# Rows of neighbouring tokens for the first two blocks of a fused channel-attention and SwiGLU kernel

## The chip, the cores and the metric

One core of a Trainium2 chip. The metric is the device time of one launch in microseconds, the median of the runs shown. The profile is one execution of the same program.

## The reference

```python
def _attn_ref(q, k, v, tau):
    qn = q / (np.linalg.norm(q, axis=1, keepdims=True) + 1e-06)
    kn = k / (np.linalg.norm(k, axis=1, keepdims=True) + 1e-06)
    s = kn.transpose(0, 2, 1) @ qn / tau
    s = s - s.max(-1, keepdims=True)
    a = np.exp(s)
    a /= a.sum(-1, keepdims=True) + 1e-09
    return (v @ a).astype(np.float32)

def _moe_ref(x, w_gate, w_val, w_out, rms_g):
    rms = np.sqrt(np.mean(x * x, axis=-1, keepdims=True) + 1e-06)
    xn = x / rms * rms_g
    g = xn @ w_gate
    silu = g * (1.0 / (1.0 + np.exp(-g)))
    val = xn @ w_val
    return (silu * val @ w_out).astype(np.float32)
```

There are two batches of 6016 tokens with 256 channels; the hidden layer has 1536 columns. q, k and v are fp32. The three weight matrices are float64 in HBM. The attention matrix is 256x256 for each batch and needs all of q and k of that batch; after it, every token stands alone.

## The kernel before

A tile is 128 tokens; a batch has 47 tiles. The work after the attention matrix runs in blocks of up to 4 tiles (`blocks`, BT = 4): eleven of 4 and one of 3 for each batch, 24 in all. The hidden layer is cut into 12 pieces of 128 columns (NF); a step is one block and one piece, (j, f). Every matmul on x, the weights and the hidden values is made of three fp32r products, of high parts and low parts (a high part is a rounding copy by ScalarE, its low part a subtraction).

**Start.** For batch 0 the scores s = k'q are summed on TensorE (`scores`, L174) over 15 chunks of q and k in three `raw` buffers, while ScalarE squares each chunk (`squares`, L189) and VectorE sums the squares (`add_squares`, L198). SP's queue loads q and k; the loads of a chunk are issued when the chunk three before it has been used. Between chunks the table `early` loads, decodes and splits the first weights: `load_w` brings a piece of all three matrices as 64-bit words (768 KB, two `wraw` buffers), `decode_w` makes fp32 of it by three operations of VectorE (L110, L119, L126) and one of ScalarE (L118), and `split_w` makes high parts (ScalarE, L134) and low parts (GpSimd, L136). v comes by `load_v` (L335) in four DMAs per block whose innermost run is 32 floats: tokens are dealt so that a VectorE transpose of 32x32 blocks (`move_v`, L366) gives v with channels on partitions. For blocks 0 and 1 these loads are issued from GpSimd's queue, the first as the first thing of the program. `split_v` makes high parts (L349) and low parts (L350, GpSimd).

**Softmax stage.** The norms, the softmax of batch 0 and the normed rows of block 0 follow: `norm_sums` (L216), `norms`, `inverse_norms`, `softmax_min`, `softmax_div`, `emit_x` (x = v a, tiles px, L386), `emit_x_squares`, `emit_xn`, `emit_xT_first` (L451). Scores of batch 1 fill TensorE's row between them (`fill`).

**Blocks 0 and 1** are plain (`emit_hidden`, L664, j < WINO = 2): six products each for pg and pv with the block's tokens as columns, then silu on ScalarE, the product hh on VectorE (L678), its high part gh on ScalarE (L553) and low part gl on GpSimd (L559). `emit_out` (L696) runs two steps later: three products per tile into po. pg and pv use four PSUM banks in turn. During block 0 the rest of batch 1's scores, and decoding and splitting of the weights of piece f + 3 and f + 2, are dealt over the steps (`weights`, `extra`).

**Blocks 2 to 23** use seven products where the plain form has eight (`new_products`, `emit_step`, L585). They need sums of weights: `build_s` makes them for pairs p of pieces in four parts i: VectorE adds high and low (part 0, L528), four additions (part 1, L537), ScalarE rounds (part 2, L540), VectorE subtracts (part 3, L543). Part i of pair p stands in step 12 + 2 + 3p + i, counted from block 0.

**Order.** The program is written by hand: an engine runs its instructions in the order written, and tables `ready0` to `ready` say in which step the next block's v, x and xT are made. With j = 0, `ready0` turns block 1's v in steps 1 and 2 (`v_moves`, `v_splits`) and makes px of block 1 at f = 4 and 6.

Of the kernel before, what the change touches and what calls it, by code (L numbers as in the profile page):

```python
# [15 lines left out]
P = 128  # L16
# [3 lines left out]
def kernel(  # L20
# [59 lines left out]
    def f32(ap):  # L80
        return ap.bitcast(F32)
# [50 lines left out]
    def split_w(f, piece=None):  # L132
        if piece in (None, 0):
            nc.scalar.activation(out=w_hl[0][:, f, :], in_=wval[f], func=AF.Copy)  # L134
        if piece in (None, 1):
            nc.gpsimd.tensor_tensor(  # L136
                out=w_hl[1][:, f, :], in0=wval.pop(f), in1=f32(w_hl[0][:, f, :]),
                op=ALU.subtract,
            )
# [188 lines left out]

    def load_v(j, queue=nc.sync):

        b, mu0, n = blocks[j]
        t = v_p.tile([P, A * BT, KC, S], F32, tag="v", name=f"v_{j}")
        src = v[b].rearrange("(s m) (c i r) -> i s m c r", s=S, c=KC, i=A)
# [5 lines left out]
        v_t[j] = t  # L339

# [96 lines left out]
    FIRST = 2  # L437

    def emit_xT_first(j, h):
# [6 lines left out]
        for c in range(KC):  # L446
# [207 lines left out]
    def emit_hidden(j, f, between=()):  # L654
# [28 lines left out]
        rounds.append((hh[:, :n], gh[:, :n], gl[:, :n], nc.gpsimd))  # L683
# [4 lines left out]
    def emit_out(j, f):  # L688
        b, mu0, n = blocks[j]
# [12 lines left out]
        if last:  # L702
# [5 lines left out]
            dst = out[b * N:(b + 1) * N, :].rearrange("(s m) e -> s m e", s=S)  # L708
            for a in range(A):
                if j < FIRST:  # L710
                    to = dst[:, mu0 + a * n:mu0 + (a + 1) * n, :]
                else:
                    to = dst[:, mu0:mu0 + A * n, :].rearrange("s (t a) e -> s t a e", a=A)[:, :, a, :]
                nc.sync.dma_start(out=to, in_=ob[S * a:S * (a + 1), :n, :])
# [3 lines left out]
    with tc.manual_schedule():  # L718
# [12 lines left out]
        load_v(0, nc.gpsimd)  # L731
# [10 lines left out]
        for i in range(6):  # L742
# [58 lines left out]
        norms(0)  # L801
        new_acc(1, 2)
# [42 lines left out]
        for f in range(NF):  # L845
# [3 lines left out]
            if f + 2 < NF:  # L849
                go.append(lambda f=f: split_w(f + 2))  # L850
# [84 lines left out]
        def rest(n):  # L935
# [30 lines left out]
            3: (then(2, v_moves),),  # L966
            4: (then(2, v_splits),),
# [84 lines left out]
```

## Time and profile before

| | us |
|---|---|
| median of 3 runs (lowest, highest) | 1321.57 (1321.02, 1322.63) |
| profiled execution, its own time | 1322.27 |
| its span, first to last instruction | 1320.4 |
| TensorE busy in the span (matmuls) | 1294.1 (98%) |
| VectorE, ScalarE, GpSimd busy | 686.1, 823.6, 679.3 |
| mean granted TensorE clock | 0.988 of full speed |

The profile shows each instruction of one execution. "Idle before" is the time an engine stood still ahead of an instruction, with what ended it. A busy TensorE is not TensorE at its peak: at half its clock it is as busy as at full.

### The profile page before, as it was taken

To read this page: it belongs to the slowest core of one execution; us is meant where nothing else is said; L and a number is where in the kernel's file an instruction comes from. 1 tells how busy PE (TensorE), PEld (TensorE's weight loads), DVE (VectorE), ACT (ScalarE), POOL (GpSimd) and SP (SyncE) were. 2 spreads that over 40 slices of the span, in tenths; PEclk is the share of its full clock that TensorE was granted. 3 is DMA by queue.
4 is the path that set the end of the run, shared out by engine and by line. 5 is a ranking of instruction groups with operands and counts; after the bars stand their busy time and mean duration, and the time that the engine had idled before them with its cause. 6 is when DMAs were issued, how large, how long until landed. Compare 5 with 4: busy or idle time off the path is not lost.

```text
span 1320.4 us, 26331 instructions
## 1 busy us (share of the span) xinstructions
PE 1294.1 (98%) x10212; PEld 1261.3 (96%) x10212; DVE 686.1 (52%) x1097; ACT 823.6 (62%) x1727; POOL 679.3 (51%) x616
## 2 busy tenths in 40 slices
PE   7999999899999999999999999999999999999998
PEld 6777888799999999999999999999999999999998
DVE  5679947753544543544643444444444444444443
ACT  4565655566657658656656666666666666666653
POOL 3226536266546546546546646646646646646432
PEclk8999999899999999999999999999999999999999
DMA  8956501202201201201201220220210210210100
GB/s 246 316 174 205 160 19 30 49 8 42 50 15 35 49 16 35 45 14 36 45 17 34 45 47 4 49 41 9 49 36 14 50 39 11 45 28 7 30 17 13
DMA packets 147678, 71.72 MB, mean 54 GB/s; under 512 B 100704, under 2 KB 139104, under 8 KB 147552
## 3 DMA queue, kind: packets, MB, share of 16 engines
q1 hardware_dynamic: 147168, 68.99, 20.3%
q0 software_dynamic: 384, 1.05, 0.5%
q8 instruction: 80, 1.31, 0.4%
q14 instruction: 46, 0.38, 0.1%
HBM read 46.40 MB, written 12.32 MB: 44 GB/s over the span
## 4 chain that ended last, share of the span: by engine, by line
PE 90%; DVE 4%; DMA 3%; ACT 1%; issue 1%; SPq 1%; ACTq 0%; DVEq 0%
PE pu L585 42%; PE po L696 29%; PE pq L585 7%; PE px L386 5%; PE s L174 3%; PE pg L664 2%; DMA raw<-in_k_dram 2%; PE pv L664 2%; DVE acc L198 1%; ACT sq L189 1%; DVE wx L119 0%; DMA raw<-in_q_dram 0%; DVE wk L537 0%; DVE s L543 0%; SPq L160 0%
## 5 line engine op out<-in xcount | busy, mean ns | idle before, releaser
L559 POOL TENSOR_TENSOR gl<-zg,gh 128x512 fp32r<-128x512 f32 (+1 forms) x262 | 327.5, 1271 | 421.5 <-ACT gh L553 220.1
L696 PE MATMUL po<-w,gh 128*128 128x256 f32 x2256 | 410.8, 280 | 0.0
L585 PE MATMUL pu<-xt,s 128*128 128x256 f32 (+1 forms) x2376 | 407.3, 280 | 0.5 <-ACT t L624 0.5
L619 ACT ACTIVATE t<-pu 128x512 f32<-128x512 f32 (+1 forms) x264 | 155.3, 588 | 372.5 <-DVE zv L613 195.2
L585 PE MATMUL pu<-xt,w 128*128 128x256 f32 (+1 forms) x2376 | 370.0, 282 | 6.2 <-DVE zg L612 5.3
L696 PEld LDWEIGHTS po<-w,gh 128*128 128x128 f32 x2256 | 348.0, 189 | 2.3 <-ACT gh L553 0.2
L585 PEld LDWEIGHTS pu<-xt,s 128*128 128x128 f32 x2376 | 336.1, 189 | 0.8 <-ACT t L624 0.7
L585 PEld LDWEIGHTS pu<-xt,w 128*128 128x128 f32 x2376 | 320.1, 189 | 7.4 <-DVE zg L612 5.9
L696 PE MATMUL po<-w,gl 128*128 128x256 f32 x1128 | 315.6, 280 | 0.1
L612 DVE TENSOR_TENSOR zv<-pu,t 128x512 f32<-128x512 f32 (+1 forms) x132 | 89.7, 680 | 336.9 <-ACT zg L632 150.4
L696 PEld LDWEIGHTS po<-w,gl 128*128 128x128 f32 x1128 | 212.9, 189 | 0.3 <-DVE gl L559 0.3
L612 DVE TENSOR_TENSOR zg<-pu,t 128x512 f32<-128x512 f32 (+1 forms) x132 | 89.7, 680 | 199.9 <-PE pu L585 189.9
L553 ACT ACTIVATE gh<-zg 128x512 fp32r<-128x512 f32 (+1 forms) x264 | 154.4, 622 | 7.3 <-DVE zg L628 4.6
L585 PE MATMUL pq<-xt,w 128*128 128x256 f32 (+1 forms) x792 | 136.1, 281 | 0.0
L628 DVE TENSOR_TENSOR zg<-zg,zv 128x768 f32<-128x768 f32 (+1 forms) x132 | 125.4, 950 | 14.4 <-DVE zv L613 0.9
L585 PEld LDWEIGHTS pq<-xt,w 128*128 128x128 f32 x792 | 111.7, 189 | 0.0
L626 ACT ACTIVATE zg<-zg 128x768 f32<-128x768 f32 (+1 forms) x132 | 109.0, 826 | 0.0
L174 PE MATMUL s<-raw 128*128 128x256 f32 x376 | 95.4, 412 | 10.6 <-DMA raw<-in_k_dram 10.6
L624 ACT ACTIVATE t<-pu 128x256 f32<-128x256 f32 (+1 forms) x264 | 100.0, 379 | 3.9 <-PE pu L585 1.3
L174 PEld LDWEIGHTS s<-raw 128*128 128x128 f32 x376 | 76.5, 208 | 25.6 <-issue 13.7
L198 DVE TENSOR_TENSOR acc<-acc,sq 128x1024 f32<-128x1024 f32 (+1 forms) x47 | 64.0, 1361 | 31.6 <-ACT sq L189 29.4
L386 PE MATMUL px<-a,vt 128*128 128x256 f32 x564 | 75.4, 283 | 0.0
(97 smaller groups left out, 1319.6 us busy)
## 6 DMA issues: line engine op xcount, KB each, us to landing
out_dram<-ob SPq DMA_DIRECT2D x88, 128.0 KB, 2.6
raw<-in_q_dram SPq DMA_DIRECT2D x20, 512.0 KB, 5.8
raw<-in_k_dram SPq DMA_DIRECT2D x20, 512.0 KB, 6.9
v<-in_v_dram SPq DMA_DIRECT2D x80, 128.0 KB, 3.8
xnT<-xw SPq DMA_DIRECT2D x320, 32.0 KB, 1.9
wraw<-in_moe_w_gate_dram SPq DMA_DIRECT2D x12, 256.0 KB, 3.5
wraw<-in_moe_w_val_dram SPq DMA_DIRECT2D x12, 256.0 KB, 4.0
wraw<-in_moe_w_out_dram SPq DMA_DIRECT2D x12, 256.0 KB, 4.8
```

The costliest lines, as they stand in the source:

```text
L174: nc.tensor.matmul(out=s_ps[b][:, c, :], lhsT=r[:, 1, t, c * P:(c + 1) * P], rhs=r[:, 0, t, :], start=(t0 + t == 0 and c == 0), stop=(t0 + ...
L198: engine.tensor_tensor(out=a, in0=a, in1=sq, op=ALU.add)
L386: nc.tensor.matmul(out=px[:, i, :], lhsT=w[:, c, t * P:(t + 1) * P], rhs=x[:, c, :], start=(i == 0 and c == 0 and m == 0), stop=(c == KC - ...
L553: nc.scalar.activation(out=gh, in_=hh, func=AF.Copy)
L559: engine.tensor_tensor(out=gl, in0=hh, in1=f32(gh), op=ALU.subtract)
L585: nc.tensor.matmul(out=out, lhsT=wm[wi], rhs=xm[xi], start=(start and q == 0), stop=(q == 2), skip_group_check=True,)
L612: nc.vector.tensor_tensor(out=z[:, 1:], in0=u, in1=t[:, :2], op=ALU.add)
L619: nc.scalar.activation(out=nt[:, 1:], in_=nu, func=AF.Copy)
L624: nc.scalar.activation(out=mt[:, 0], in_=mu[:, 1], func=AF.Copy)
L626: nc.scalar.activation(out=zg[:, 1:], in_=zg[:, 1:], func=AF.Silu)
L628: nc.vector.tensor_tensor(out=zg[:, 1:], in0=zg[:, 1:], in1=z, op=ALU.mult)
L696: nc.tensor.matmul(out=o_ps[j][t // 2][:, t % 2, :], lhsT=g[:, t * P:(t + 1) * P], rhs=wo[w][:, f, :], start=(first and t % 2 == 0 and m = ...
```

## The change

Tokens of blocks 0 and 1 are now neighbouring tokens of batch 0. Their v is loaded in rows by one DMA from SP's queue (`load_v_rows`, 3 or 4 KB a partition), turned by TensorE with the identity into PSUM (`turn_v`, tiles pvt) and split out of PSUM by ScalarE and VectorE (`split_turned`). Block 0 has 3 tiles in place of 4, and block 11 has 4 in place of 3. In block 0 the low parts gl and the low parts of the weights are made by VectorE. The first weights are loaded some chunks later, v of block 0 late in the chunks, v of block 1 after the softmax. The parts of `build_s` stand in other steps.

```diff
-    def split_w(f, piece=None):
...
-            nc.gpsimd.tensor_tensor(
-                out=w_hl[1][:, f, :], in0=wval.pop(f), in1=f32(w_hl[0][:, f, :]),
...
+    def split_w(f, engine=nc.gpsimd):
+        nc.scalar.activation(out=w_hl[0][:, f, :], in_=wval[f], func=AF.Copy)
+        engine.tensor_tensor(
+            out=w_hl[1][:, f, :], in0=wval.pop(f), in1=f32(w_hl[0][:, f, :]), op=ALU.subtract,
+        )
...
-            n = min(BT, NT - t)
+            n = (NT - t) % BT or BT if b == 0 else min(BT, NT - t)
...
+    def load_v_rows(j):
+        n = blocks[j][2]
+        v_t[j] = v_p.tile([P, A * BT, KC, S], F32, tag="v", name=f"v_{j}")
+        nc.sync.dma_start(
+            out=v_t[j].rearrange("p m c r -> p (m c r)")[:, :n * C],
+            in_=v[0, rows(j), :].rearrange("(p t) c -> p (t c)", p=P),
+        )
+
+    def turn_v(j, c, psum, tag):
+        n = blocks[j][2]
+        x = v_t[j].rearrange("p m c r -> p (m c r)")
+        v_w[j, c] = psum.tile([P, BN], F32, tag=tag, name=f"pvt_{j}_{c}")
+        for t in range(n):
+            nc.tensor.transpose(
+                v_w[j, c][:, t * P:(t + 1) * P], x[:, t * C + c * P:t * C + (c + 1) * P], ident
+            )
+
+    def split_turned(j, c):
+        n = blocks[j][2] * P
...
+        split(v_w.pop((j, c))[:, :n], [x[:, c, :n] for x in vT[j]])
...
-        rounds.append((hh[:, :n], gh[:, :n], gl[:, :n], nc.gpsimd))
+        rounds.append((hh[:, :n], gh[:, :n], gl[:, :n], nc.gpsimd if j else nc.vector))
...
-        load_v(0, nc.gpsimd)
...
         early = {
-            2: lambda: load_w(0),
-            5: lambda: (load_w(1), decode_w(0)),
-            6: lambda: split_w(0),
-            8: lambda: (load_w(2), decode_w(1)),
-            9: lambda: split_w(1),
-            12: lambda: load_w(3),
+            4: lambda: load_w(0),
+            7: lambda: (load_w(1), decode_w(0)),
+            8: lambda: split_w(0),
+            10: lambda: load_v_rows(0),
+            11: lambda: (load_w(2), decode_w(1)),
+            12: lambda: split_w(1),
+            13: lambda: load_w(3),
         }
...
-            if i == 3:
-                move_v(0, 0)
-                move_v(0, 1)
-                for c in range(KC):
-                    split_v(0, c, nc.gpsimd)
-                load_v(1, nc.gpsimd)
+        for c in range(KC):
+            turn_v(0, c, ps_gv, "u")
...
         norms(0)
+        for c in range(KC):
+            split_turned(0, c)
...
             softmax_div(0, c)
+        load_v_rows(1)
...
-                go.append(lambda f=f: split_w(f + 2))
+                go.append(lambda f=f: split_w(f + 2, nc.vector))
...
-        for i in reversed(range(4)):
+        at_step = [(2 * p + 2, 2 * p + 3, 2 * p + 3, 2 * p + 4) for p in range(NP - 2)]
+        at_step += [(10, 11, 12, 13), (15, 18, 19, 20)]
+        for i in (3, 0, 1, 2):
             for p in range(NP):
-                j, f = divmod(NF + 2 + 3 * p + i, NF)
+                j, f = divmod(NF + at_step[p][i], NF)
...
-            3: (then(2, v_moves),),
-            4: (then(2, v_splits),),
+            4: (then(2, v_moves),),
+            5: (then(2, v_splits),),
...
         ready0 = {
-            1: (v_moves,),
-            2: (v_splits,),
+            0: (turn(0),),
+            1: (turned(0),),
+            2: (turn(1),),
+            3: (turned(1),),
```

The output of blocks 0 and 1 goes out by one DMA in place of four (L708 to L714), and the loads and stores of batch 0's other blocks leave out the first 896 tokens. `ready2` moves block 4's v by one step.

**SP's queue in the first stage.** Of the kernel before, the loads behind chunk 5 (raw is q and k, wraw a piece of the weights):

```order
L96 DMA wraw_202<-in_moe_w_gate_dram 128x2x256
L96 DMA wraw_202<-in_moe_w_val_dram 128x2x256
L100 DMA wraw_202<-in_moe_w_out_dram 128x512
L160 DMA raw_6_220<-in_q_dram 128x1024
L160 DMA raw_6_220<-in_k_dram 128x1024
L160 DMA raw_7_251<-in_q_dram 128x1024
L160 DMA raw_7_251<-in_k_dram 128x1024
```

Of the change, the same place:

```order
L157 DMA raw_6_211<-in_q_dram 128x1024
L157 DMA raw_6_211<-in_k_dram 128x1024
L157 DMA raw_7_228<-in_q_dram 128x1024
L157 DMA raw_7_228<-in_k_dram 128x1024
L96 DMA wraw_231<-in_moe_w_gate_dram 128x2x256
L96 DMA wraw_231<-in_moe_w_val_dram 128x2x256
L100 DMA wraw_231<-in_moe_w_out_dram 128x512
```

The first weights stand behind two more chunks. The second piece moves from behind chunk 8 to behind chunk 10, the third from behind chunk 11 to behind chunk 14, the last of batch 0; v of block 0 stands between chunks 13 and 14.

**VectorE's row in block 0, one step.** Of the kernel before, step f = 0 (wx is a piece of weights in decoding, hh the hidden values, acc the sums of squares of batch 1):

```order
L110 TENSOR_SCALAR wx_608<-wraw_400 128x768
L678 TENSOR_TENSOR hh_0_606<-th_0_605,pv_0_598 128x512
L119 SCALAR_TENSOR_TENSOR wx_608<-wraw_400,wx_608 128x768
L126 SCALAR_TENSOR_TENSOR wx_608<-we_611,wx_608 128x768
L198 TENSOR_TENSOR acc_435<-acc_435,sq_2_2_629 128x1024
```

Of the change, the same step:

```order
L110 TENSOR_SCALAR wx_597<-wraw_393 128x768
L713 TENSOR_TENSOR hh_0_595<-th_0_594,pv_0_587 128x384
L119 SCALAR_TENSOR_TENSOR wx_597<-wraw_393,wx_597 128x768
L134 TENSOR_TENSOR w_101<-wx_534,w_100 128x768
L126 SCALAR_TENSOR_TENSOR wx_597<-we_600,wx_597 128x768
L594 TENSOR_TENSOR gl_0_611<-hh_0_595,gh_0_610 128x384
L195 TENSOR_TENSOR acc_432<-acc_432,sq_2_2_623 128x1024
```

Two operations are added to each step, the low parts of the weights (L134) and of the hidden values (L594), and GpSimd's row loses them. In steps 1 and 3 a subtraction for block 1's v (vt) follows behind gl.

**VectorE's row in block 1, two steps.** Of the kernel before, f = 4 to 6 (zh is the hidden product, wk and s are the parts of `build_s`, vw block 3's v):

```order
L678 TENSOR_TENSOR zh_4_1570<-zh_4_1570,pv_4_1563 128x512
L678 TENSOR_TENSOR zh_5_1606<-zh_5_1606,pv_5_1599 128x512
L543 TENSOR_TENSOR s_1439<-wk_1457,s_1438 128x512
L543 TENSOR_TENSOR s_1439<-wk_1457,s_1438 128x256
L543 TENSOR_TENSOR w_101<-wk_1457,w_100 128x256
L528 TENSOR_TENSOR wk_1612<-w_100,w_101 128x512 x2
L366 STREAM_TRANSPOSE vw_1631<-v_1148 128x4x4x32 x2
L678 TENSOR_TENSOR zh_6_1653<-zh_6_1653,pv_6_1646 128x512
```

Of the change:

```order
L713 TENSOR_TENSOR zh_4_1530<-zh_4_1530,pv_4_1523 128x512
L578 TENSOR_TENSOR s_1396<-wk_1414,s_1395 128x512
L578 TENSOR_TENSOR s_1396<-wk_1414,s_1395 128x256
L578 TENSOR_TENSOR w_101<-wk_1414,w_100 128x256
L563 TENSOR_TENSOR wk_1536<-w_100,w_101 128x512 x2
L713 TENSOR_TENSOR zh_5_1569<-zh_5_1569,pv_5_1562 128x512
L572 TENSOR_TENSOR wk_1536<-wk_1536 128x256 x4
L403 STREAM_TRANSPOSE vw_1595<-v_1123 128x4x4x32 x2
L713 TENSOR_TENSOR zh_6_1617<-zh_6_1617,pv_6_1610 128x512
```

A pair is built in two steps in place of three, and ScalarE's rounding (part 2) now stands in the step of part 1. Of the 24 parts, eight stood in the first six steps of block 2 before; of the change three stand there.

## Rows read from the trace of the kernel before

**Rows 1.** Stages: us of stage, busy time (x count) by engine, granted clock, DMA share, GB/s.
```profile
0.00:61.35 61.35, 51.39 (x200) 41.98 (x201) 37.28 (x34) 29.97 (x32) 15.84 (x21) 0.89 0.89 273
61.35:84.30 22.95, 21.17 (x106) 17.66 (x107) 13.28 (x30) 10.57 (x25) 3.83 (x6) 0.93 0.57 205
84.30:172.10 87.80, 84.91 (x441) 73.77 (x441) 79.47 (x68) 54.89 (x84) 50.72 (x30) 0.96 0.55 169
172.10:228.00 55.90, 55.90 (x335) 49.25 (x334) 34.50 (x46) 27.97 (x62) 30.03 (x27) 1.00 0.14 29
228.00:265.00 37.00, 30.62 (x223) 29.41 (x223) 29.23 (x50) 21.83 (x50) 11.97 (x10) 0.91 0.21 44
```

**Rows 2.** The same view, two stretches of the first stage.
```profile
10.00:20.00 10.00, 9.08 (x22) 6.78 (x23) 5.33 (x5) 4.95 (x5) 0.00 (x0) 0.53 0.88 300
30.00:40.00 10.00, 7.30 (x28) 5.93 (x27) 5.41 (x6) 4.66 (x5) 2.51 (x1) 0.83 1.03 266
```

**Rows 3.** Waits of TensorE in 0 to 62 us: in total, times, longest.
```profile
PE s L174 <- DMA raw<-in_k_dram: 7.7, 5, 2.7
```

**Rows 4.** GpSimd's DMA queue in 0 to 62 us: packets, MB, share of 16 engines.
```profile
q0 software_dynamic: 384, 1.05, 10.3%
```

**Rows 5.** TensorE's timeline, turns and scores in block 0: start, us, instruction, count.
```profile
155.98 0.60 PE L451 MATMUL pxt<-ident,xn 128*128 128x128 f32 x4
156.42 3.62 PE L174 MATMUL s<-raw 128*128 128x256 f32 x16
159.68 1.75 PE L664 MATMUL pg<-xt,w 128*128 128x512 f32 x6
```

**Rows 6.** TensorE's timeline, one plain step of 4 tiles in block 1.
```profile
191.45 1.57 PE L664 MATMUL pg<-xt,w 128*128 128x512 f32 x6
192.85 1.56 PE L664 MATMUL pv<-xt,w 128*128 128x512 f32 x6
194.25 0.40 PE L696 MATMUL po<-w,gh 128*128 128x256 f32 x2
...
195.65 1.57 PE L664 MATMUL pg<-xt,w 128*128 128x512 f32 x6
```

**Rows 7.** TensorE's timeline, products of 256 and of 192 columns.
```profile
683.09 0.51 PE L585 MATMUL pu<-xt,s 128*128 128x256 f32 x3
683.44 0.52 PE L585 MATMUL pq<-xt,w 128*128 128x256 f32 x3
...
691.63 0.83 PE L585 MATMUL pu<-xt,w 128*128 128x192 f32 x6
692.30 0.50 PE L585 MATMUL pu<-xt,s 128*128 128x192 f32 x3
```

**Rows 8.** VectorE's groups by shape, whole span: busy us, mean ns, idle before.
```profile
L628 DVE TENSOR_TENSOR zg<-zg,zv 128x768 f32<-128x768 f32 x120 | 116.2, 968 | 13.2 <-DVE zv L613 0.9
L559 DVE TENSOR_TENSOR gl<-zg,gh 128x384 fp32r<-128x384 f32 x2 | 1.0, 556 | 0.3 <-ACT gh L553 0.3
```

**Rows 9.** VectorE's timeline, softmax stage (first three) and step 0 of block 0.
```profile
73.47 1.22 DVE L198 TENSOR_TENSOR acc<-acc,sq 128x1024 f32<-128x1024 f32 x1
...
78.78 0.55 DVE L110 TENSOR_SCALAR wx<-wraw 128x768 uint32<-128x768 uint32 x1
79.37 0.96 DVE L119 SCALAR_TENSOR_TENSOR wx<-wraw,wx 128x768 uint32<-128x768 uint32 x1
...
85.75 2.56 DVE L198 TENSOR_TENSOR acc<-acc,sq 128x1024 f32<-128x1024 f32 x2 [0.46 <-ACT sq L189]
...
89.60 2.50 DVE L119 SCALAR_TENSOR_TENSOR wx<-wraw,wx 128x768 uint32<-128x768 uint32 x1
92.20 1.86 DVE L126 SCALAR_TENSOR_TENSOR wx<-we,wx 128x768 uint32<-128x768 uint32 x1
```

**Rows 10.** Waits of TensorE in 228 to 265 us, the longest group.
```profile
PE pu L585 <- DVE zg L612: 5.3, 3, 2.5
```

**Rows 11.** VectorE's timeline at one of these waits, in block 2.
```profile
241.22 3.19 DVE L537 TENSOR_TENSOR wk<-wk 128x256 f32<-128x256 f32 x4
```

More of the change, by code (lines that the diff above doesn't have):

```diff
@@ L130, in decode_w @@
             wval[f] = x.bitcast(F32)
-    def split_w(f, piece=None):
-        if piece in (None, 0):
-            nc.scalar.activation(out=w_hl[0][:, f, :], in_=wval[f], func=AF.Copy)
-        if piece in (None, 1):
-            nc.gpsimd.tensor_tensor(
-                out=w_hl[1][:, f, :], in0=wval.pop(f), in1=f32(w_hl[0][:, f, :]),
-                op=ALU.subtract,
-            )
+    def split_w(f, engine=nc.gpsimd):
[3 more added lines that the diff above has]
+        )
     CH = 4
@@ L315 @@
     A = P // S
-    MU = N // S
+    FIRST = 2
     blocks = []
@@ L324 @@
     NB = len(blocks)
+    ROWS = sum(n for _, _, n in blocks[:FIRST]) * P
     B1 = NB // B
@@ L329, in load_v @@
     def load_v(j, queue=nc.sync):
-        b, mu0, n = blocks[j]
+        n = blocks[j][2]
+        r, mu0 = strided(j)
         t = v_p.tile([P, A * BT, KC, S], F32, tag="v", name=f"v_{j}")
-        src = v[b].rearrange("(s m) (c i r) -> i s m c r", s=S, c=KC, i=A)
+        src = v.rearrange("b n c -> (b n) c")[r].rearrange(
+            "(s m) (c i r) -> i s m c r", s=S, c=KC, i=A
+        )
         for i in range(A):
@@ L339, in load_v, with rows, strided @@
         v_t[j] = t
+    def rows(j):
+        r = blocks[j][1] * S
+        return slice(r, r + blocks[j][2] * P)
+    def strided(j):
+        b, mu0, _ = blocks[j]
+        skip = 0 if b else ROWS
+        return slice(b * N + skip, (b + 1) * N), mu0 - skip // S
+    def load_v_rows(j):
[6 more added lines that the diff above has]
+    def turn_v(j, c, psum, tag):
+        n = blocks[j][2]
+        x = v_t[j].rearrange("p m c r -> p (m c r)")
[3 more added lines that the diff above has]
+                v_w[j, c][:, t * P:(t + 1) * P], x[:, t * C + c * P:t * C + (c + 1) * P], ident
+            )
+    def split_turned(j, c):
+        n = blocks[j][2] * P
+        if c == 0:
+            vT[j] = [vt_p.tile([P, KC, BN], F32R, tag=f"vt{i}", name=f"vt{i}_{j}") for i in range(2)]
+        split(v_w.pop((j, c))[:, :n], [x[:, c, :n] for x in vT[j]])
     def half_tiles(j, h):
@@ L435, in new_xT @@
         xp[j] = [x[:, :XS * n // 2].rearrange("p (i n) -> p i n", i=XS) for x in t]
-    FIRST = 2
     def emit_xT_first(j, h):
@@ L452, in emit_xT_first @@
             parts.append((
-                ps[:, c].rearrange("p t n -> p (t n)"), [x[:, c, cols] for x in xT[j]],
+                ps[:, c, :len(ts)].rearrange("p t n -> p (t n)"), [x[:, c, cols] for x in xT[j]],
                 g_sb[:, c:c + 1],
@@ L688, in emit_out @@
     def emit_out(j, f):
-        b, mu0, n = blocks[j]
+        n = blocks[j][2]
         first, last = f == 0, f == NF - 1
@@ L707, in emit_out @@
                 nc.scalar.activation(out=o, in_=o_ps[j][h][:, :len(ts), :], func=AF.Copy)
[L708 to L714, printed above, removed]
+            if j < FIRST:
+                nc.sync.dma_start(
+                    out=out[rows(j), :].rearrange("(p t) e -> p t e", p=P), in_=ob[:, :n, :]
+                )
+            else:
+                r, mu0 = strided(j)
+                dst = out[r, :].rearrange("(s m) e -> s m e", s=S)[:, mu0:mu0 + A * n, :]
+                dst = dst.rearrange("s (t a) e -> s t a e", a=A)
+                for a in range(A):
+                    nc.sync.dma_start(out=dst[:, :, a, :], in_=ob[S * a:S * (a + 1), :n, :])
             del o_ps[j]
@@ L987, with turn, turned @@
         }
+        def turn(c):
+            return lambda n: turn_v(n, c, ps_m, "m")
+        def turned(c):
+            return lambda n: split_turned(n, c)
         ready0 = {
-            1: (v_moves,),
-            2: (v_splits,),
+            0: (turn(0),),
+            1: (turned(0),),
+            2: (turn(1),),
+            3: (turned(1),),
             4: (x(0), squares_of_x(0)),
```

## Prediction

> **What bounds the kernel now.** I read the busy times first: TensorE works 98% of the span, so only two things can be won, time in which it stands or runs at half clock, and columns. The stages [rows 1] say where the first lies: up to 265 us TensorE is idle for 21 us (265 less the five busy times, 243.98), and in four of the five stages the granted clock is under 1.00. One less the clock, times the length, is a loss of its own: 6.7 us in the first stage, 1.6 in the softmax stage, 3.5 in block 0, 3.3 at the start of block 2. Block 1 loses nothing. From 265 us on TensorE runs through.
>
> The first stage waits for q and k: five waits, 7.7 us, the longest 2.7 [rows 3]. The DMA engines are full there (share 0.89), and 1.05 MB of v, in runs of 32 floats from GpSimd's queue, holds 10.3% of 62 us, 6.4 us of all sixteen engines [rows 4]; at the 273 GB/s of the stage the same bytes would be 3.8 us. The clock is at 0.53 from 10 to 20 us and at 0.83 from 30 to 40, where TensorE also stood 2.7 us [rows 2].
>
> In block 0 VectorE is busy 79.47 of 87.8 us [rows 1], but much of that is waiting beside GpSimd: L119 takes 0.96 us in the softmax stage and 2.50 in step 0, L126 1.86 [rows 9]. TensorE still sets the pace: it is idle for 2.89 us only.
>
> At the start of block 2 TensorE waits for VectorE, 5.3 us in three waits [rows 10], whose row holds parts of `build_s` ahead of the sums that TensorE needs: four L537 take 3.19 us at one of the waits [rows 11].
>
> **The change, part by part.** The sum is made against the profiled execution, 1322.27 us (span 1320.4 and 1.87 around it), 0.7 above the median.
>
> *1. The first stage, to the norm sums at 61.35 us.* Block 0's v no longer shares the engines with the first chunks: half of 6.4, 3.2 us. The longest wait (2.7) has block 1's v and the first weights ahead of its chunk; both leave, and with the wait goes its low clock, (1 - 0.83) x 10 = 1.7. Of the other waits about 1.0 more. That is 8.6. Against it: decoding of the second piece (0.55 + 0.96 + 0.96 = 2.5 us [rows 9]) now stands between the last sums of squares, on the chain that ends the stage; its cost is 0 to 2.5, and I take 0.6, since ScalarE's squares run beside it. Bytes do not forbid it: raw (12.3 MB), two pieces of weights (1.6) and v (0.4) are 14.3 MB in place of 15.7, and at the 273 GB/s of the stage [rows 1] the missing 1.4 MB alone are 5 us. Forecast -8.0; bounds -11 (all waits and the clock of 30 to 40 us) and -3 (block 0's v alone).
>
> Six turns are put ahead of the norm sums. Four turns of the same shape take 0.44 us, 155.98 to 156.42 [rows 5], so six take 0.7, in time in which TensorE waits for the last squares: nothing; 0.7 if that cover is gone. The Trainium skill, "VectorE: DVE Perf Modes", section "The three transpose paths", gives 390 ns for a TensorE turn of 128x128 (in bf16): by that figure, as an estimate, the 14 turns of both blocks would cost 5.5 us and not 1.5. It speaks against turning on the busiest engine, and the row bears it out only for a turn that stands alone.
>
> *2. Softmax stage.* px of block 0 has 18 products for 24, 6 x 0.117 = 0.7 us by the price of 256 columns [rows 7]; ScalarE squares one tile less. Two subtractions out of PSUM (556 ns each by the 384-column row of gl [rows 8]) are put on VectorE where it waits for GpSimd's power, and SP gets one more load. Forecast -1.0; bounds -3 (all idle and half the clock loss) and +1.5 (both subtractions and one clock step exposed).
>
> *3. Block 0, 87.8 us.* Columns: six products of 512 take 1.40 us [rows 6], 0.234 each; 256 columns take 0.35 / 3 = 0.117 [rows 7], so 384 take 0.176, and 144 products lose 0.058 each, 8.4 us. 36 out products of 0.117 (twelve take 1.40 [rows 6]) go: 4.2. Eight turns for block 1 come: 0.9. Sum -11.7.
> Then VectorE. With GpSimd silent its operations should cost what they cost alone: L110 0.55, hh 0.56, L119 0.96, the weights' low part 0.97 (the 768-column row), L126 0.96, gl 0.56 and 1.5 sums of squares of 1.22 [rows 8, 9]: 6.4 us a step. TensorE's step is 2.1 (pg, pv) + 1.05 (po) + 1.5 parts of scores at 1.63 (half of 156.42 to 159.68 [rows 5]) = 5.6. Over nine decoding steps VectorE falls 7 us behind; four PSUM banks and the two steps until po allow about that. Two places have less room. The second turn (f = 2) needs the bank of the first, whose subtraction is behind step 1's whole row: VectorE gets there at 15 us from the block's start (4.0 until the two sums at 85.75 are done [rows 9], step 0 with one sum 5.8, the operations of step 1 4.6, the subtraction 0.6), TensorE at 12.6 (steps of 2.1 + 1.6 and 2.1 + 3.3, then 3.15 and a turn of 0.4). px of block 1 (f = 4) needs the second subtraction: 28.5 against 26.5 by the same walk. With 2 us of low clock after two such waits and 0.5 elsewhere, block 0 loses 7 us, where it now loses 2.9 + 3.5 = 6.4: +0.6. Forecast -11; bounds -16 (no wait, full clock) and -4 (a step of 7.2 us).
>
> *4. Block 11, 3 tiles to 4.* A product of 192 columns takes 0.67 / 6 = 0.112, one of 256 0.117 [rows 7]: the fourth tile costs 252 x 0.005 = 1.4 us in the products, because the weight load sets their pace. 36 out products and six of px at 0.117 add 4.9. Together +6.4, bounds 5.9 and 6.9. This is the point of the tiles: 3 tiles are cheap as columns of 512 and dear as halves.
>
> *5. Block 2's start.* Lost there now: 37 - 30.62 = 6.4 us and 3.3 of clock, 9.7. Of eight parts in the first six steps three stay. The other five move into block 1, where VectorE has 34.5 of 55.9 us taken [rows 1] and, at up to 3.19 us a part, gets 8 to 16 more: it fits on the whole, tightly in steps of 4.2 us (191.45 to 195.65 [rows 6]). ScalarE's rounding now waits there for the four additions of its own step, ahead of gh, and po two steps later has a few us of room. I leave 3.4 us for new waits. Forecast -6.3; bounds -9.7 and -1.
>
> The rest costs nothing: one store for four, and one load on SP's queue for four on GpSimd's, hidden by TensorE's running through.
>
> Sum: -8.0 - 1.0 - 11 + 6.4 - 6.3 = -19.9; 1322.3 - 19.9 = **1302 us**.
>
> **The rivals.**
> *A. The start does not follow the loads.* Clock and the serial row of squares and sums hold the stage; only block 0's v is won, -3: 1307. For it: the clock at 0.53 from 10 to 20 us, which no load explains alone. Against it: the waits name q and k. Chance 0.12.
> *B. VectorE sets block 0's pace.* A step of 7.4 us, nine steps, 9 us more: 1311. For it: VectorE's long rows; against it: 0.96 alone. 0.12.
> *C. Slower.* The two operations that GpSimd gave up each wait for a copy by ScalarE, and ScalarE's next square waits for VectorE's sum; if they take turns, every step of block 0 holds both. From a step of 9.0 us (2.6 more, nine times, 23) all of the gain is gone; with a wait per pair in block 1 beside it: 1326. Against it: in the written order ScalarE makes each copy before VectorE comes to it, the weights' one behind work that is a step old. 0.03.
> *D. Every turn stands alone.* Then the 14 cost 4 us more, as none of the fill is shared: 1306. Against it: the four in 0.44 us. 0.05.
> *E. Both stalls go whole*, first stage -11, block 2 -9.7, one wait less in block 0: 1294. 0.08.
> My forecast keeps 0.60.
>
> **How the numbers follow.** What a measurement can tell from no change is 0.2%, 2.6 us. The terms' bounds lie some 7 us either side of the sum when not all fall together; A, B and D lie inside 1312, E inside 1293. So 1293 to 1312 leaves out C, the far half of B and sums beyond both ends, 0.2. Faster by over 0.2% (under 1319): everything but C and the worst of B, 0.95; within 0.2%: 0.02; slower: 0.03.
>
> **What would show it.** In the profile after: norm sums near 53 us, waits for k under 3 us, no v on the software queue; L119 at 0.96 in block 0, whose length is 75 to 78 us with waits at the second turn and at px; VectorE's share there over 0.9; 128x192 rows gone before the last block; no wait over 1 us at the start of block 2. I am wrong if block 0 stays over 82 us, if block 1 shows waits of more than 4 us, or if the norm sums come after 57 us.

## The result, and the profile after

| us | before | after |
|---|---|---|
| median (lowest, highest), four runs each | 1321.41 (1321.02, 1322.63) | 1306.66 (1303.99, 1309.74) |
| profiled execution | 1322.27 | 1304.33 |

The ratio is 0.9888 with an interval of 0.9859 to 0.9916: faster by 1.1%. The median lies in the range that was forecast, 1293 to 1312, 4.7 us above the forecast itself, 1302: 14.8 us are won between the medians and 18 between the two profiled executions, for 19.9 forecast. The terms are judged against the profiled executions, one of each kernel; how far the stages of the changed kernel vary is in runs 1 and 12. The marks below are from their timelines. For the last two rows they are ScalarE's copies of the output (`ob`): the gain is 24.8 us at those of block 2 (273.44 for 298.28) and 18.2 at those of block 12 (769.82 for 788.02).

| mark | before | after | difference | forecast |
|---|---|---|---|---|
| norm sums | 61.35 | 52.80 | -8.55 | -8.0 |
| from there to block 0's first pg | 22.95 | 20.93 | -2.0 | -1.0 |
| block 0, to block 1's first pg | 87.80 | 74.20 | -13.6 | -11 |
| block 1 and the start of block 2, to the end of block 2 (what is left) | | | -0.67 | -6.3 |
| block 11 (from the end of block 2 to that of block 12) | | | +6.6 | +6.4 |

The stages of the changed kernel, cut at the same marks; to be read against [rows 1]:

```profile
0.00:52.80 52.80, 46.73 (x207) 39.28 (x207) 35.08 (x32) 29.17 (x31) 6.01 (x11) 1.00 0.86 295
52.80:73.73 20.93, 18.62 (x98) 15.82 (x99) 14.20 (x32) 10.42 (x24) 4.67 (x6) 1.00 0.77 277
73.73:147.93 74.20, 72.60 (x419) 68.59 (x419) 67.72 (x90) 51.87 (x84) 6.00 (x6) 0.98 0.65 199
147.93:203.83 55.90, 55.41 (x329) 48.56 (x328) 36.95 (x54) 26.67 (x59) 26.78 (x24) 1.00 0.12 27
203.83:241.00 37.17, 30.45 (x231) 29.60 (x230) 28.72 (x43) 22.91 (x54) 16.45 (x14) 0.86 0.21 44
```

Four stages stand at 0.98 to 1.00 of full clock. In the last, the start of block 2, TensorE is idle for 6.7 us of 37 at 0.86. That is the stage from which 6.3 us were to come, and the waits say what is there now. TensorE's waits in 0 to 260 us of the changed kernel (in total, times, longest):

```profile
PE s L171 <- DMA raw<-in_k_dram: 6.6, 8, 2.0
PE pu L620 <- ACT t L654: 5.6, 1, 5.6
...
PE pu L620 <- ACT t L659: 1.0, 1, 1.0
```

The three waits for VectorE's zg, 5.3 us [rows 10], are gone, and one wait of 5.6 us for ScalarE's t stands in their place. The granted clock behind it is 0.87 from 200 to 210 us and 0.62 from 210 to 220, by the same sum of (1 - clock) x 10 another 5.1 us.

What made ScalarE late is in three timelines of the changed kernel. ScalarE, at the end of block 1:

```profile
198.29 0.63 ACT L575 ACTIVATE s<-wk 128x512 fp32r<-128x512 f32 x1 [5.09 <-DVE wk L572]
...
200.51 0.61 ACT L588 ACTIVATE gh<-zh 128x512 fp32r<-128x512 f32 x1
...
209.07 0.63 ACT L588 ACTIVATE gh<-zh 128x512 fp32r<-128x512 f32 x1 [3.77 <-DVE zh L713]
...
210.32 0.60 ACT L654 ACTIVATE t<-pu 128x512 f32<-128x512 f32 x1
```

VectorE over the same time:

```profile
196.97 3.19 DVE L572 TENSOR_TENSOR wk<-wk 128x256 f32<-128x256 f32 x4
...
203.34 2.37 DVE L578 TENSOR_TENSOR s<-wk,s 128x512 fp32r<-128x512 f32 x2
205.63 1.48 DVE L578 TENSOR_TENSOR w<-wk,w 128x256 fp32r<-128x256 f32 x1
207.15 1.29 DVE L563 TENSOR_TENSOR wk<-w,w 128x512 f32<-128x512 f32 x2
208.36 0.68 DVE L713 TENSOR_TENSOR zh<-zh,pv 128x512 f32<-128x512 f32 x1
...
213.14 0.42 DVE L578 TENSOR_TENSOR w<-wk,w 128x256 fp32r<-128x256 f32 x1
```

And GpSimd:

```profile
202.44 2.99 POOL L545 TENSOR_TENSOR xt<-xp,xt 128x512 fp32r<-128x512 f32 x2
205.39 1.44 POOL L594 TENSOR_TENSOR gl<-zh,gh 128x512 fp32r<-128x512 f32 x1
```

ScalarE stands 5.09 us in front of the rounding of `build_s` (L575), whose additions (L572) VectorE makes in that same step, and gh (L588) is queued behind it. Then VectorE has 5.1 us of `build_s` ahead of the last zh, part of it stretched beside GpSimd's parts of block 2's x (L545) and a low part gl (L594): L578 on 128x256 takes 1.48 us beside that gl, and 0.42 at 213.14, when GpSimd is quiet. It is not that block 1 as a whole had no room: VectorE is busy there for 36.95 us, 2.5 more than the 34.50 of before [rows 1]. The last gh waits 3.77 us for that zh, and the first t of block 2 stands behind this gh on ScalarE.

Block 0 is the opposite. VectorE's groups there by shape (busy us, mean ns, idle before), two of the kernel before and then four of the changed one:

```profile
L126 DVE SCALAR_TENSOR_TENSOR wx<-we,wx 128x768 uint32<-128x768 uint32 x9 | 16.8, 1861 | 0.9
L119 DVE SCALAR_TENSOR_TENSOR wx<-wraw,wx 128x768 uint32<-128x768 uint32 x9 | 16.2, 1799 | 0.0
```
```profile
L134 DVE TENSOR_TENSOR w<-wx,w 128x768 fp32r<-128x768 f32 x10 | 9.5, 952 | 0.0
L119 DVE SCALAR_TENSOR_TENSOR wx<-wraw,wx 128x768 uint32<-128x768 uint32 x9 | 8.6, 953 | 0.0
L126 DVE SCALAR_TENSOR_TENSOR wx<-we,wx 128x768 uint32<-128x768 uint32 x9 | 8.6, 952 | 0.0
L594 DVE TENSOR_TENSOR gl<-hh,gh 128x384 fp32r<-128x384 f32 x12 | 6.6, 553 | 1.2 <-ACT gh L588 1.2
```

L119 and L126, 1.80 and 1.86 us on average before, are 0.95 each with GpSimd nearly silent (busy for 6.0 us of the block, 50.7 before). VectorE does 22 operations more in 12 us less of busy time (67.7 for 79.5); part of that is the smaller block, and run 4 has the comparison with three tiles on both sides.

I expected a wait at the second turn. Both turns in TensorE's timeline of block 0, and VectorE's subtraction between them:

```profile
77.30 0.78 PE L368 MATMUL pvt<-ident,v 128*128 128x128 f32 x4
...
88.38 0.60 PE L368 MATMUL pvt<-ident,v 128*128 128x128 f32 x4
```
```profile
86.59 0.68 DVE L387 TENSOR_TENSOR vt<-pvt,vt 128x512 fp32r<-128x512 f32 x1
```

The subtraction ends (87.27) 1.1 us before the second turn: no wait, nor is there one at px.

### The profile page after: what moved, and what is told of

Its sections match the earlier page's. It is cut to its first block, busy times and chain, and to the rows that moved or that the text cites. A ratio compares the mean times of both kernels' runs of the same rounds, so it can differ in the third digit from the quotient of the medians.

```text
span 1302.2 us, 26312 instructions
## 1 busy us (share of the span) xinstructions
PE 1279.6 (98%) x10224; PEld 1256.9 (97%) x10224; DVE 679.4 (52%) x1119; ACT 825.0 (63%) x1727; POOL 633.3 (49%) x582
## 3 DMA queue, kind: packets, MB, share of 16 engines
q1 hardware_dynamic: 148512, 70.17, 20.8%
## 4 chain that ended last, share of the span: by engine, by line
PE 88%; DVE 5%; DMA 3%; ACT 2%; issue 2%; SPq 0%; ACTq 0%; DVEq 0%
PE pu L620 43%; PE po L731 29%; PE pq L620 7%; PE px L423 5%; DMA raw<-in_k_dram 3%; PE s L171 3%; PE pg L699 1%; PE pv L699 1%; DVE wk L572 1%; DVE w L578 0%; DVE zh L713 0%; DVE wx L119 0%; DVE s L578 0%; DVE wx L126 0%; ACT sq L186 0%
## 5 line engine op out<-in xcount | busy, mean ns | idle before, releaser
L594 POOL TENSOR_TENSOR gl<-zg,gh 128x512 fp32r<-128x512 f32 (+1 forms) x262 | 331.1, 1285 | 420.8 <-ACT gh L588 224.7
L588 ACT ACTIVATE gh<-zg 128x512 fp32r<-128x512 f32 (+1 forms) x264 | 155.4, 627 | 6.8 <-DVE zg L663 4.2
L171 PE MATMUL s<-raw 128*128 128x256 f32 x376 | 86.7, 385 | 6.8 <-DMA raw<-in_k_dram 6.6
L171 PEld LDWEIGHTS s<-raw 128*128 128x128 f32 x376 | 70.7, 192 | 18.6 <-issue 6.8
L448 POOL TENSOR_SCALAR ss<-ss 128x2 f32<-128x2 f32 (+1 forms) x48 | 11.4, 237 | 123.4 <-ACT xn L439 123.0
```

Of the source, the lines that this page charges most:

```text
L171: nc.tensor.matmul(out=s_ps[b][:, c, :], lhsT=r[:, 1, t, c * P:(c + 1) * P], rhs=r[:, 0, t, :], start=(t0 + t == 0 and c == 0), stop=(t0 + ...
L588: nc.scalar.activation(out=gh, in_=hh, func=AF.Copy)
L594: engine.tensor_tensor(out=gl, in0=hh, in1=f32(gh), op=ALU.subtract)
```

## The experiments

The kernel before ran beside each group, on its chip: 1321.78, 1320.36, 1321.19 and 1321.74 us (medians of 7 to 11 runs) in the four groups. So times within a group compare directly, and across groups by ratio. I call "b0 to b2" the time from the first copy of block 0's output to that of block 2's: 117.4 us before, 117.1 after.

**1. The changed kernel again** (`same`; no edit).

> The changed kernel itself, as a base for the other runs on this chip, and to see whether its runs lie in two groups, near 1304 and near 1309 us, as its first four did. Theory 1: a stall at the start of block 2 (5.6 us in the profile, with 5.1 us of low clock behind it) falls longer or shorter by how VectorE and GpSimd meet there; then a second profile shows another length of that stall, and the first stage (norm sums at 52.8 us), block 0 (74.2 us) and the blocks from 3 on stay within 0.5 us. Theory 2: the loads of the first stage vary; then the norm sums come some 5 us later in a profile of a slower run.

1308.19 us, ratio 0.9897 (0.9882 to 0.9911). Norm sums at 52.80 and the wait of 5.6 us at block 2's start, both as in the first profile, but block 0 starts at 77.42 and not at 73.73. Two stretches of the softmax stage, the first profile and then this one:

```profile
54.00:58.00 4.00, 3.39 (x19) 3.04 (x19) 2.85 (x9) 1.06 (x1) 1.93 (x2) 1.00 1.04 393
58.00:62.00 4.00, 4.00 (x20) 3.52 (x19) 2.88 (x7) 2.18 (x5) 0.00 (x0) 1.00 0.99 352
```
```profile
54.00:58.00 4.00, 2.66 (x12) 2.24 (x12) 2.85 (x9) 1.06 (x1) 1.93 (x2) 0.66 1.02 404
58.00:62.00 4.00, 4.00 (x11) 3.19 (x10) 0.93 (x1) 0.00 (x0) 0.00 (x0) 0.50 1.04 378
```

Here the first chunk of batch 1 came 0.7 us later (56.09 for 55.35), TensorE was idle for 1.3 us, and it was granted half its clock for the 16 products behind. This stage takes 24.6 us here and 20.9 in the first profile, 3.7 of the 4.7 us between the two executions; it is neither of the two causes that I had named. In the seven profiles of kernels that share this stage (this one, the first, runs 2, 4, 7, 9 and 12) it takes between 20.9 and 24.6 us, 23.4 on average: no gain against the 22.95 of the one profile of before. The norm sums, by the same seven, come at 52.6 to 55.6 us, 53.6 on average.

**2. `build_s` by its old step table** (`old_table`).

```
-        at_step = [(2 * p + 2, 2 * p + 3, 2 * p + 3, 2 * p + 4) for p in range(NP - 2)]
-        at_step += [(10, 11, 12, 13), (15, 18, 19, 20)]
-        for i in (3, 0, 1, 2):
+        for i in reversed(range(4)):
...
-                j, f = divmod(NF + at_step[p][i], NF)
+                j, f = divmod(NF + 2 + 3 * p + i, NF)
```

> The changed kernel with the parts of the weight sums (build_s) back in the steps they had before; the rest as changed. Theory 1: the new table only moved the stall from the first steps of block 2 into its first step, because ScalarE's rounding waits for the four additions of its own step: lost there now 7 us of waits and 5 of clock, before 6.4 and 3.3. Expected then 2 us faster to equal, 1302 to 1306, with waits of TensorE for VectorE's sums 14 to 30 us into block 2 and none of 5 us at its first step. Rival: the new table is worth what was forecast, 6 us: 1310 or more, and two or three waits that add up to over 9 us.

1308.35 us, ratio 0.9895 (0.9878 to 0.9912); b0 to b2 117.0. Its wait:

```profile
PE pu L620 <- DVE zg L647: 6.7, 3, 4.6
```

The old table brings back the wait for VectorE, and the time is the same as that of the changed kernel beside it, within the intervals. The new table moved the stall from one engine to another and is worth nothing by itself that these runs can tell.

**3. Block 0 with four tiles** (`four_first`).

```
-            n = (NT - t) % BT or BT if b == 0 else min(BT, NT - t)
+            n = min(BT, NT - t)
```

> The changed kernel with block 0 of 4 tiles again and the 3-tile block last in batch 0, as before. Theory 1 (columns): block 0 has 144 products of 512 for 384 columns (0.058 us each) and 36 more output products, 13.3 us with px; the 3-tile block saves 6.6 by the two profiles; 7 us slower, 1311 to 1313. Rival (VectorE sets block 0's pace): block 0's step is VectorE's 6.4 us and not TensorE's, so 4 tiles cost it less than 10 us and the whole is at most 3 us slower.

1310.55 us, 2.4 above the changed kernel in the group. Block 0 from its first pg to the copies, this run and then the changed kernel again:

```profile
77.32:169.67 92.35, 92.35 (x499) 80.93 (x499) 75.94 (x95) 59.12 (x94) 7.01 (x9) 0.98 0.53 160
```
```profile
77.42:160.74 83.32, 79.71 (x466) 74.30 (x466) 72.13 (x95) 55.65 (x94) 8.20 (x9) 1.00 0.59 178
```

TensorE's busy time differs by 12.6 us, as much as the 8.4 + 4.2 of the prediction, but that agreement is partly chance: in its first step this run was granted 0.66 of full clock (77.32 to 82.32), and pg and pv took 4.4 us there. Steps at full clock show the columns themselves, with four tiles in this run and with three in the first profile of the change:

```profile
83.72 1.76 PE L699 MATMUL pg<-xt,w 128*128 128x512 f32 x6
85.31 1.56 PE L699 MATMUL pv<-xt,w 128*128 128x512 f32 x6
86.71 3.62 PE L171 MATMUL s<-raw 128*128 128x256 f32 x16
```
```profile
79.46 1.41 PE L699 MATMUL pg<-xt,w 128*128 128x384 f32 x6
80.70 1.22 PE L699 MATMUL pv<-xt,w 128*128 128x384 f32 x6
81.76 3.61 PE L171 MATMUL s<-raw 128*128 128x256 f32 x16
```

From start to start pg and pv take 2.99 and 2.30 us, 8.3 us over twelve steps for the 8.4 of the prediction.

The stage differs by 9.0 us only. With three tiles the block waits for k in this pair (four waits, 3.6 us, all of what TensorE is idle); with four it waits for nothing. That the shorter block is what brings these waits is not shown: the kernel before, with four tiles, waited 2.9 us for k there, and the longer block of run 4 waits 4.3. Less the 6.6 us that block 11 costs, 9.0 leaves 2.4, as measured.

**4. The low parts back on GpSimd in block 0** (`pool_low`).

```
-        rounds.append((hh[:, :n], gh[:, :n], gl[:, :n], nc.gpsimd if j else nc.vector))
+        rounds.append((hh[:, :n], gh[:, :n], gl[:, :n], nc.gpsimd))
...
-                go.append(lambda f=f: split_w(f + 2, nc.vector))
+                go.append(lambda f=f: split_w(f + 2))
```

> The changed kernel with the low parts of block 0's hidden values and of its weights made by GpSimd again. Theory 1: beside GpSimd VectorE's decoding takes 1.6 to 2.5 us an operation in place of 0.96, so its step goes from 6.4 us to over 7 although it does two operations less, TensorE's step is 5.6, and block 0 grows from 74 us to 80 or more: 1310 to 1316. Rival: VectorE's wait beside GpSimd is cover, TensorE keeps the pace as it did before the change; within 2 us of the changed kernel.

1314.26 us, 6.1 above, and block 0 is 6.1 us longer (89.45 for 83.32). VectorE's decoding and TensorE's waits in that block:

```profile
L119 DVE SCALAR_TENSOR_TENSOR wx<-wraw,wx 128x768 uint32<-128x768 uint32 x9 | 16.8, 1869 | 0.0
L126 DVE SCALAR_TENSOR_TENSOR wx<-we,wx 128x768 uint32<-128x768 uint32 x9 | 14.3, 1585 | 0.9
```
```profile
PE s L171 <- DMA raw<-in_k_dram: 4.3, 4, 1.9
PE px L423 <- DVE vt L387: 1.7, 1, 1.7
PE pxt L486 <- DVE xt L393: 1.1, 1, 1.1
PE pvt L368 <- DVE vt L387: 0.5, 1, 0.5
```

With GpSimd at work VectorE's decoding takes 1.9 and 1.6 us again, and the waits at the turn and at px that I forecast for the change are there. Moving the work to the busier engine is what keeps them away. From block 0's first pg to block 1's VectorE is busy for 73.2 us with 68 operations here, and for 67.8 us with 90 in the changed kernel run again.

**5. The weights early again** (`early_old`): `load_w(0)` to `load_w(3)` at steps 2, 5, 8, 12 with their decoding and splitting, v in rows at its new place.

```
-            4: lambda: load_w(0),
-            7: lambda: (load_w(1), decode_w(0)),
+            2: lambda: load_w(0),
+            5: lambda: (load_w(1), decode_w(0)),
...
```

> The changed kernel with one part undone: weights 0 to 2 are loaded, decoded and split two to three chunks earlier again (v in rows stays at its place). Theory 1 (each of the two causes of the first stage's gain, weights later and v in rows later, is worth about half of it): the norm sums come at 56 to 58 us in place of 52.8, waits for k grow by 2 to 4 us, and the time is 3 to 5 us above 1308. Rival a (it was v's strided load alone): norm sums at 53 to 54, time within 1.5 us. Rival b (it was the weights alone): norm sums at 60 or later and the clock falls again at 10 to 20 us, time 7 to 9 us above.

1306.47 us, ratio 0.9898 (0.9881 to 0.9914), no different from the changed kernel's. Norm sums at 54.01, 1.2 us later; waits for k up to there 6.9 us for 4.5. Rival a; but 1.2 us is less than the norm sums differ between profiles of one order (52.6 to 55.6), so a price of the weights is not shown.

**6. A strided load of v ahead of the first chunks** (`v_strided`); four transfers, read by nothing.

```
...
+        load_v(2, nc.gpsimd, xn_p, "moved")
         for i in range(RAW):
```

> The changed kernel with one load more: 512 KB of v in runs of 32 floats from GpSimd's queue ahead of the first chunks, as block 0's v was before the change; nothing reads it. Theory 1: it takes 3 us of all DMA engines, the norm sums come 3 to 4 us later (56 to 57 us) and the time rises by 3 to 5 us. Rival a (it also starves TensorE enough for the low clock of 10 to 20 us, 0.53 before the change): norm sums 5 to 9 us later. Rival b (the loads have room there): under 1 us.

1312.88 us, ratio 0.9941 (0.9926 to 0.9956). Waits for k up to the norm sums 7.2 us for 4.5, and the sums themselves:

```profile
56.62 1.05 PE L213 MATMUL pn<-ones,sq 128*128 128x1 f32 x8 [0.71 <-ACT sq L186]
```

3.8 us later than 52.80, and 1.1 later than the latest of the seven profiles without this load; the time is longer too, by 0.4% (ratio 0.9941 for 0.9897). So the load costs something, and how much is uncertain by some 3 us. The kernel before had two such loads in this stage, the changed one has one of 384 KB in rows in their place. Two of them and the weights' 1.2 make 8.8, an estimate from two profiles, for the 8.55 won. The clock from 10 to 20 us was 0.83, and 1.00, 1.00 and 0.66 in the three profiles of the changed kernel.

**7. ScalarE's rounding behind gh** (`round_later`): in block 1 part 2 goes to the end of its step.

```
-                if j == 1:
+                if j == 1 and i != 2:
```

> The changed kernel, with one part of build_s moved: in block 1 ScalarE's roundings (part 2) are written at the end of their step, behind the step's gh, and no longer ahead of it. Theory 1 (the wait at the start of block 2, 5.6 us with 5.1 us of low clock behind it, comes from ScalarE standing 5.09 us before gh for VectorE's four additions of the same step): gh no longer waits, the wait at the first step of block 2 is under 1.5 us, the clock there stays at 1.00, and the time falls by 6 to 10 us against the changed kernel run again (1308.2), to 1299 to 1302. Rival (VectorE's own row, stretched beside GpSimd, is what is late there; ScalarE only shows it): the wait stays at 4 us or more and the time within 2 us of 1308.

1305.53 us, ratio 0.9887 (0.9873 to 0.9902). The wait falls from 5.6 to 4.2 us, where I expected under 1.5, b0 to b2 falls to 114.8, and the clock behind the wait is still low (0.66 from 210 to 220 us). About half of theory 1: the place in the order cost some 2.5 us. As the rival has it, VectorE's own row is late as well: the last gh still waits 3.1 us for zh.

**8. Weights 2 and 3 later** (`w_late`): `load_w(2)` behind the loop over the chunks of batch 0, `load_w(3)` behind `load_v_rows(1)`.

> The changed kernel, with the weights 2 and 3 (1.5 MB) loaded behind the first three chunks of k and q of batch 1 instead of between the last chunks of batch 0 and these. Theory 1 (these bytes hold up batch 1's first chunk; the wait for it, 0.6 to 1.3 us at 55 us, is what sometimes throws the clock to 0.50 for 6 us): waits for raw before 62 us fall by 2 us or more, the clock from 54 to 62 us stays above 0.95, block 0 starts by 73 us, and the time is 3 to 6 us under that of the changed kernel run again (1308.2). Rival (the DMA engines are full there whatever the order, and the weights only come late instead): the saved wait returns at the decoding of weights 2 or 3, and the time is within 1.5 us of 1308.

1307.32 us, ratio 0.9904 (0.9889 to 0.9918): nothing. Block 0 starts at 75.04, TensorE is busy throughout 54 to 62 us, and the granted clock there is 0.78 and 0.79 all the same. So the wait for the chunk is not all that comes before a low clock there. Ahead of the norm sums TensorE had stood 1.2 us for a square, where the first profile shows 0.47, and the norm sums themselves are 16 products of a single column; which of these matters was not tried.

**9. Another table for `build_s`** (`clear_end`; on top of 7).

```
-        at_step = [(2 * p + 2, 2 * p + 3, 2 * p + 3, 2 * p + 4) for p in range(NP - 2)]
-        at_step += [(10, 11, 12, 13), (15, 18, 19, 20)]
+        at_step = [(2, 2, 2, 3), (3, 4, 4, 5), (5, 6, 6, 7), (7, 8, 8, 9)]
+        at_step += [(13, 14, 15, 16), (17, 18, 19, 20)]
```

> The changed kernel with another step table for build_s: four pairs are done by step 9 of block 1, nothing of it in steps 10 and 11 and in step 0 of block 2, pairs 4 and 5 from step 1 of block 2 on; ScalarE's roundings stand behind gh as in the run before. Theory 1 (what was left of the wait there, 4.2 us, is VectorE's row: 8 us of build_s between the h of steps 9 and 11, on which gh and, behind it on ScalarE, the first t of block 2 wait): the wait at block 2's first step falls to 2 us or less, the low clock behind it goes, block 2 ends 3 to 6 us sooner after block 0's end than with the roundings moved alone (114.8 us), and the time is 1299 to 1303. Rival a (the parts moved into block 2 make VectorE late there, as before the change): new waits for zg or zv of 3 us or more in block 2, time 1304 to 1309. Rival b (the first t waits for GpSimd's power and ScalarE's scaling of block 3's x, not for VectorE): the wait stays above 3.5 us.

1304.67 us, ratio 0.9872 (0.985 to 0.9894); the wait is 2.8 us, b0 to b2 113.7. The direction of theory 1, but 1.1 us where I asked for 3; no new wait in block 2 above 0.6 us.

**10. Both, 8 and 9** (`clear_late`).

> The same with the weights 2 and 3 loaded behind the first chunks of batch 1 as well. Theory 1 (this order is worth only what the clock at 54 to 62 us happens to lose, 0 to 3 us): within 2.5 us of the run above, block 0 begins at 73.5 to 76 us. Rival (the two add up, since the wait for the first chunk of batch 1 is what throws the clock): 3 to 5 us under it.

1302.45 us, ratio 0.9859 (0.9838 to 0.9879), 2.2 below the run beside it: theory 1, and with overlapping intervals. b0 to b2 112.5. Left is a wait of 2.7 us, behind a scaling (L464) for which ScalarE waits 1.56 us for GpSimd's power.

**11. The first t ahead of that scaling** (`t_first`; on top of 10).

```
-            0: (squares_of_x(1),),
+            0: (xn(0), squares_of_x(1)),
...
-            11: (then(2, xn(0)),),
```

> The last version (other step table, weights 2 and 3 later), with ScalarE's scaling of block 3's first x tiles (L464) moved from the end of block 1's step 11 behind the first step of block 2, so that it no longer stands ahead of the first t. Theory 1 (the 2.7 us left there are ScalarE waiting 1.56 us for GpSimd's power in front of that scaling, and the scaling itself, 0.84): the wait at block 2's first step goes under 0.8 us, no low clock follows it, block 0's end to block 3's start of the copies falls from 112.5 us to 108 to 110, and the time is 2 to 4 us under the last version's 1302.5. Rival (something else is as late, the h of step 11 or GpSimd's low part of it): the wait stays above 2 us and the time within 1.5 us.

1301.82 us, ratio 0.9845 (0.9832 to 0.9858); b0 to b2 113.3, so nothing is won there. The waits in the start of block 2:

```profile
PE pu L620 <- ACT t L659: 2.4, 1, 2.4
...
PE pu L620 <- ACT t L654: 0.4, 1, 0.4
```

The first half of t is in time, and the second half now stands behind the same scaling, one step on: ScalarE still waits 1.07 us there for GpSimd's power, which is queued behind x's low parts (L545) and a gl. Moved, not removed: the third time at this place.

**12. The changed kernel on the chip of 11** (`again`; no edit).

> The changed kernel once more, on the same chip, to compare with. Theory 1 (its runs differ among themselves only by what the clock loses around 54 to 62 us): 1304 to 1310 us, norm sums at 52.6 to 53.2, the wait at block 2's start 5.6 us as before. Rival (chips differ): the kernel before stands elsewhere than at 1321 too.

1309.74 us, ratio 0.9913 (0.9901 to 0.9925). The wait is 5.6 us and b0 to b2 117.4, as in both other profiles, but the norm sums came at 55.55: TensorE waited 3.3 us for k ahead of 11.7 us, where the other two waited 2.0 and 2.3, and the clock was 0.66 from 10 to 20 us. So that the first stage keeps its clock, as in the first profile of the change, is not sure. Block 0 took 76.9 us here, 74.2 and 74.9 in the other two. The version of 11 is 7.9 us faster than the change on the same chip, with separate intervals; some 4 us of it are between the blocks' ends, the rest is not pinned to an edit. One candidate is the later load of weights 2 and 3, which run 8 alone did not show: in its three profiles (runs 8, 10 and 11) the softmax stage takes 20.8 to 22.4 us, 21.7 on average, for 23.4 in the seven without it.

## Why the prediction was right, and where not

- *What bounds it.* Right: what was won is waiting, low clock and columns before 265 us, and from there on TensorE runs through in both kernels.
- *First stage, -8.0 forecast, -8.55 measured* (-8.55 and -5.8 in runs 1 and 12). Right in size; the shares are open. I gave v's load 3.2 us and the rest to the longest wait, its clock and the weights. By one profile each, one strided load is worth 3.8 us (run 6) and the weights 1.2 (run 5), and the norm sums differ by 2.8 us between profiles of the changed kernel itself. The low clock that I counted, 0.83 from 30 to 40 us, is gone in all three profiles of the changed kernel (1.00); that of 10 to 20 us, 0.53 before, is 1.00, 1.00 and 0.66. Rival A, 1307 for a start that does not follow the loads, would have had the norm sums at 58.4 us; they came before that in every profile.
- *Turns, 0.* Right: six take 0.82 us, 51.51 to 52.33, where TensorE then still waits 0.47 us for a square. Rival D falls with it. The Trainium skill, "VectorE: DVE Perf Modes", section "The three transpose paths", gives 390 ns for a turn of 128x128 in bf16. The traces, in fp32, do not agree: six in a row take 0.82 us, and a turn that stands alone takes 0.30 (at 81.93 us in the kernel before). That the row bears the price out for a turn alone, as I had written, was a misreading: [rows 5] show no such turn.
- *Softmax stage, -1.0.* -2.0 in the first profile, +1.7 and +0.4 in the two later ones; the runs differ by more here than the term was worth. That may be why the median lies 2.3 us above the profiled execution.
- *Block 0, -11 forecast, -13.6 measured* (-12.9 and -10.9 in runs 1 and 12). The columns are right: 8.3 us for 8.4 by the steps in run 3. What was wrong is "VectorE falls 7 us behind", with waits at the second turn and at px. I had a step of 6.4 us for VectorE and 5.6 for TensorE; the first steps took 6.1 (77.44 to 101.88 us, four steps) and 5.9 (73.73 to 103.30, five). VectorE had done the subtraction 13.5 us from the block's start, where I had said 15, and TensorE came to the turn at 14.7, where I had said 12.6: the clock was 0.73 from 75 to 80 us, and its first pg and pv took 3.6 us, for 2.3 in the second step. In run 1 the clock was full there and a wait of 1.3 us for k came instead; the turn was at 14.6 us all the same. So rival B was refuted as well. And I put the low parts on VectorE at about nothing, when without that move the three tiles would have lost 6.1 us of their gain (run 4).
- *Block 11, +6.4.* Measured +6.6, by the rows of a 192 and a 256 column product. My sum was loose: 252 x 0.005 is 1.3 and not 1.4, and with the 4.9 the rows give +6.2.
- *Block 2's start, -6.3 forecast, about -0.7 measured.* This step failed: "it fits on the whole", with 3.4 us left for new waits. They came to all of it: 5.6 + 1.0 us and a low clock behind them. I had named the wait, "ScalarE's rounding now waits there for the four additions of its own step, ahead of gh", but counted VectorE's room over the whole block. There was more than enough of that: VectorE got 2.5 us more in block 1, not 8 to 16. The last three steps decide: there GpSimd makes block 2's x and stretches VectorE's parts, and block 2's first t stands behind the last gh. Run 7 shows 2.5 us for ScalarE's place in the order and run 9 another 1.1 for VectorE's row; what is left is a wait behind ScalarE's scaling and GpSimd's power (runs 10 and 11).
- *The signs that I named.* Norm sums near 53 us, L119 at 0.96, VectorE's share of block 0 over 0.9 (67.72 of 74.20): as said. Waits for k in the first stage came to 4.5 us, not under 3; block 0 was shorter than 75 to 78 us in two of three profiles and had none of the two waits; a wait of 5.6 us stood at block 2's start, where I had said none over 1, one step behind the block 1 in which I would have counted it as a sign of being wrong.
- *The sum.* Two misses of 2.6 and 5.6 us of opposite sign and one of 1.0 left 17.9 for 19.9. That the total came out so near owes something to luck.

## What to carry to other kernels

A piece of work that is moved to an engine "with room" has to be laid against the steps where it lands, and above all the last ones before a change of stage: what stands behind it in the same queue decides, not the engine's share of busy time over the block. When a stall changes its name in the waits (zg, then t, then the other half of t) but the distance between two fixed marks stays, it was moved; measure that distance, not the wait. And when two engines slow each other, giving the work of the idle one to the busy one can be the cheaper order: in block 0 VectorE did 22 operations more in 5.4 us less of busy time, and the stage was 6.1 us shorter (run 4).

## What was not expected of the hardware

- VectorE's 128x768 operation on whole numbers takes 0.95 us with GpSimd nearly silent and 1.6 to 1.9 on average beside it (run 4), and single ones 2.50 [rows 9].
- The granted clock may fall, or not, at the same place of the same program: 1.00 or 0.50 at 58 to 62 us, 1.00 or 0.66 at 10 to 20 us, in three profiles of the changed kernel. Where it fell, a longer wait for k stood in front (1.3 and 1.4 us for 0.6 at batch 1's first chunk, 3.3 for 2.0 and 2.3 at 11 us). In run 8 it stood at 0.78 with TensorE busy throughout. Differences of some 3 to 4 us between profiles go with it.
- Half a megabyte more, in runs of 32 floats, went with norm sums 3.8 us later (run 6, one profile). At 295 GB/s, the rate of the changed kernel's first stage, the bytes alone are 1.8 us, an estimate; whether the rest is the short runs, the clock or chance, no run tells.
